# Batch 0's products in a ring of five, its stages B and P on other PSUM banks, z written in six pieces, and stage Y and B units of batch 1's time in other slots

## The chip, the cores and the metric

The kernel runs on one core of one Trainium2 chip. The metric is the time on the device in microseconds (us), from the median of several runs. A profiled run gives a trace besides; its span is about 2 us shorter than the time of the same run. Engine names: PE is TensorE, DVE is VectorE, ACT is ScalarE, POOL is GpSimd, SP is the queue that issues nearly all DMA transfers.

## The reference

```python
def _attn_ref(x, filt_r, filt_i):            # x: 8 x 3008 x 256
    X = np.fft.rfft(x, axis=1)
    Y = X * (filt_r + 1j * filt_i)[None]
    return np.fft.irfft(Y, n=x.shape[1], axis=1)

def _moe_ref(x, w_in, w_out):                # 24064 tokens, 256 -> 2048 -> 256
    h = np.maximum(x @ w_in, 0.0)
    return h * h @ w_out
```

A filter in the frequency domain along the sequence, then a feed-forward network (FFN) with a squared ReLU, over eight batches.

## The kernel before

3008 = 64 x 47, so the transform is done by matmuls in stages. The kernel keeps matmul results in a few tiles of one or two banks of PSUM each, which it uses again and again; a stage that takes a tile waits until the stage before it has been read out. For each batch: **A** (short transforms, result `u` to DRAM and back as `ut`), **B** (second transforms), a **product** with the filter on DVE, **P** (back transforms; ACT evicts them, that is, copies them out of PSUM, as `ze`, which is written to DRAM as `z` and read back in four chunks as `zt`), **Y** (last transforms, giving the tokens `yt`). The FFN goes over 47 groups of 512 tokens in eight slots each: a slot is four matmuls `psH` (w_in), eight matmuls `psO` (w_out, of the group before), a ReLU eviction on ACT and a square on DVE. Batch 0 is transformed in a prologue; the transforms of batch b+1 are strewn over the slots of batch b's FFN by a plan.

The parts that matter (cuts marked with `# ...`):

```python
p_prod = ctx.enter_context(tc.tile_pool(name="p_prod", bufs=3))   # 2 KB per partition each
p_ze = ctx.enter_context(tc.tile_pool(name="p_ze", bufs=3))
# ...
def psF(name):      # two banks; stages A, B, P and Y take them in turn (batch 0's P is on psO)
    return pps.tile([128, 512], F32, tag="psF", name=name, bufs=2)
# psO: two tiles of one bank; psH: two tiles of two banks
sPF = p_prod.tile([128, 6, 128], F16, tag="prod", name="sPF")     # sits in one product buffer

def unit_b(b, p):
    ps = psF(f"psB_{b}_{p}")
    # two matmuls, then on DVE:
    prod = p_prod.tile([128, 2, 2, D], F16, tag="prod", name=f"prod_{b}_{p}")
    nc.vector.tensor_mul(out=prod, in0=..., in1=sF[:, :, 2 * p:2 * p + 2, :])

def fft_plan(b):                       # put(slot, place, unit, ...); place 0 is before psO
    if b == 1:
        for n in range(4, 16):         # the rest of batch 0's stage Y
            put(n - 1 if n < 8 else 10 + n // 2 if n < 12 else 4 * n - 31, n % 2, unit_y, 0, n)
    # ...
    for p in range(12):
        r = t0 + 19 * p // 11          # t0 = 14 for batch 1
        put(r, 0, unit_b, b, p)
        put(r, 0, unit_s, b, p)
        put(r + 2, 1, unit_p, b, p)
    t0 = 36 if b == 1 else 40
    for c in range(4):
        put(t0, 1, read_z, b, c)

# prologue, after the filter's first parts are placed:
for r in range(14):
    if r < 12: unit_b(0, r)
    if r < 10 and r % 2 == 0: place_f(1, r // 2 + 1, nc.scalar)
    if r in (1, 3): place_f(0, r // 2 + 4, nc.scalar)
    if r >= 2: unit_p(0, r - 2)
    for k in {4: (1,), 7: (2,)}.get(r, ()):
        load_wide(1, k); cast_wide(1, k, nc.gpsimd, nc.gpsimd)   # 1 MB of x for batch 1
    if r == 10: read_z(0, 0, (0,))
read_z(0, 0, (1,))
for k in range(2): load_wout(k)        # 2 MB
read_z(0, 1)
```

## Time and profile before

| | before |
|---|---|
| time, median of 3 runs | 809.09 us (808.6 to 809.66) |
| span of the profiled run | 806.2 us |
| PE busy | 784.3 us |
| first stage Y matmul of batch 0 | 52.43 us |
| slot 0, 8, 14, 18, 39 of the FFN begin at | 54.32, 65.48, 77.66, 89.85, 133.11 us |

How to read it: PE is nearly always busy, so the question is only where its idle time lies and what each piece of it waits for. The begin of a slot is the begin of its first `psH` matmul in the timeline. These begins are a ruler: the difference between two of them, held against the same difference in another trace, tells in which stage time was won.

### The profile page before, as it was taken

The numbers are of one execution on the slowest core, as the hardware profiler recorded it, in microseconds if no ns is written. First come the engines' busy times: TensorE is split into PE (matmuls) and PEld (weight loads), VectorE is DVE, ScalarE is ACT, GpSimd is POOL, SyncE is SP. The second block draws the span as 40 slices with busy tenths as digits, with TensorE's granted clock in tenths as the row PEclk, the third lists the DMA queues.
The fourth block names the chain that finished last, engine by engine and source line by source line (L and its number), as shares of the span: only waits on it lengthen the run. The fifth ranks groups of instructions, "written<-read, shape, count | busy, mean of one in ns | idle before, by whom it ended". The sixth has DMA issues, their size and how long they took to land.

```text
span 806.2 us, 14778 instructions
## 1 busy us (share of the span) xinstructions
PE 784.3 (97%) x6102; PEld 552.4 (69%) x6102; DVE 554.1 (69%) x899; ACT 554.0 (69%) x709; POOL 18.5 (2%) x23
## 2 busy tenths in 40 slices
PE   8879899999999999999999999999999999999997
PEld 5746566767776676866768677776667667676666
DVE  6756896569955798558975599656995579654342
ACT  3756666767767677676767677777777767666663
POOL 3320000000000000000000000000000000000000
PEclk9999999999999999999999999999999999999999
DMA  9895357155543457235671555625563332511111
GB/s 362 315 280 177 91 153 176 55 169 144 154 109 82 142 157 198 65 105 157 163 178 39 174 138 138 155 66 157 143 170 91 98 126 82 128 52 41 40 40 53
DMA packets 88091, 108.10 MB, mean 134 GB/s; under 512 B 6240, under 2 KB 78816, under 8 KB 83552
## 3 DMA queue, kind: packets, MB, share of 16 engines
q1 hardware_dynamic: 87816, 106.98, 46.4%
q8 instruction: 48, 0.79, 0.4%
q10 hardware_dynamic: 144, 0.18, 0.1%
q14 instruction: 19, 0.16, 0.1%
q0 software_dynamic: 64, 0.00, 0.0%
HBM read 58.90 MB, written 48.23 MB: 133 GB/s over the span
## 4 chain that ended last, share of the span: by engine, by line
PE 87%; DMA 6%; DVE 4%; ACT 1%; issue 0%; SPq 0%; ACTq 0%; DVEq 0%
PE psO L549 37%; PE psH L534 36%; DMA zt<-dZ 3%; PE psA L349 3%; PE psB L433 3%; PE psY L504 2%; DMA ut<-dU 2%; PE psP L468 2%; DVE prod L436 2%; DMA dZ<-ze 1%; PE warm L267 1%; PE psf L283 1%; ACT h L538 0%; PE psf L286 0%; DVE h L542 0%
## 5 line engine op out<-in xcount | busy, mean ns | idle before, releaser
L538 ACT ACTIVATE h<-psH 128x1024 f16<-128x1024 f32 x376 | 384.8, 1024 | 193.2 <-PE psH L534 193.2
L534 PE MATMUL psH<-yt,sWin 128*128 128x512 f16 (+7 forms) x1728 | 387.8, 352 | 2.8 <-DVE yt L513 2.2
L549 PE MATMUL psO<-sWout,h 128*128 128x256 f16 x3008 | 388.7, 273 | 0.0
L549 PEld LDWEIGHTS <-h 128*128 128x128 f16 x3008 | 290.2, 98 | 78.2
L542 DVE TENSOR_TENSOR h<-h 128x1024 f16<-128x1024 f16 x376 | 254.3, 685 | 105.6 <-ACT h L538 104.1
L534 PEld LDWEIGHTS <-sWin 128*128 128x128 f16 x1728 | 159.3, 98 | 103.5 <-issue 5.3
L436 DVE TENSOR_TENSOR prod<-psB,sF 128x1024 f16<-128x1024 f32 x96 | 116.6, 1219 | 10.9 <-PE psB L433 7.4
L513 DVE CAST yt<-psY 128x376 f16<-128x376 f32 x64 | 35.0, 549 | 59.3 <-PE psY L504 59.3
L470 ACT CAST ze<-psP 128x512 f16<-128x512 f32 x96 | 55.8, 585 | 22.8 <-PE psP L468 19.4
L355 DVE CAST u<-psA 96x512 f16<-96x512 f32 x50 | 34.3, 687 | 47.3 <-PE psA L349 45.1
L556 ACT COPY ost<-psO 128x512 f32<-128x512 f32 x94 | 55.4, 590 | 8.1 <-PE psO L549 6.4
L504 PE MATMUL psY<-sC,zt 112*128 112x94 f16 x512 | 42.8, 207 | 5.2 <-DMA zt<-dZ 5.2
L504 PEld LDWEIGHTS <-zt 112*128 112x128 f16 x512 | 35.0, 99 | 17.6 <-DMA zt<-dZ 5.6
L433 PE MATMUL psB<-ut,sSB 128*128 128x256 f16 x192 | 36.7, 272 | 3.3 <-DVE prod L436 1.9
L450 DVE TENSOR_TENSOR yf<-prod,yf 128x512 f16<-128x512 f16 x84 | 35.7, 425 | 2.9
L349 PE MATMUL psA<-x,sC 94*96 94x512 f16 x96 | 36.7, 382 | 0.0
L433 PEld LDWEIGHTS <-sSB 128*128 128x128 f16 x192 | 18.6, 97 | 24.9 <-issue 6.2
L468 PE MATMUL psP<-yf,sSP 128*128 128x256 f16 x168 | 32.1, 273 | 1.8 <-DVE prod L436 1.6
L511 ACT CAST yt<-psY 128x376 f16<-128x376 f32 x64 | 29.8, 468 | 3.9 <-PE psY L504 3.9
L328 DVE CAST x<-x 94x2048 f16<-94x2048 f32 x24 | 29.2, 1216 | 0.0
L353 ACT CAST u<-psA 96x512 f16<-96x512 f32 x50 | 28.6, 572 | 0.0
L443 DVE COPY yf<-prod 64x512 f16<-64x512 f16 x84 | 24.3, 289 | 2.9
(59 smaller groups left out, 227.2 us busy)
## 6 DMA issues: line engine op xcount, KB each, us to landing
x<-in_x_dram SPq DMA_DIRECT2D x20, 768.0 KB
dZ<-ze SPq DMA_DIRECT2D x32, 384.0 KB
zt<-dZ SPq DMA_DIRECT2D x64, 192.0 KB
dU<-u SPq DMA_DIRECT2D x28, 384.0 KB
out_dram<-ost SPq DMA_DIRECT2D x32, 256.0 KB
out_dram<-ost SPq DMA_DIRECT2D x64, 128.0 KB
ut<-dU SPq DMA_DIRECT2D x7, 1024.0 KB
xw<-in_x_dram SPq DMA_DIRECT2D x6, 1024.0 KB
```

What stands on the lines that cost most here:

```text
L349: nc.tensor.matmul(ps[0:96, :], sSA, x16s[(b, c)][:, m, :], start=True, stop=True)
L433: nc.tensor.matmul(ps[:, i * D:(i + 1) * D], sSB[:, 2 * p + i, :], uts[b][:, 2 * p + i, :], start=True, stop=True)
L436: nc.vector.tensor_mul(out=prod, in0=ps.rearrange("p (a d) -> p a d", d=D).unsqueeze(1).to_broadcast([128, 2, 2, D]), in1=sF[:, :, 2 * p:2 ...
L450: nc.vector.tensor_add(out=yf, in0=prod[:, 0], in1=yf)
L468: nc.tensor.matmul(ps[:, i * D:(i + 1) * D], sSP[:, c2, :], prod[:, i, :], start=True, stop=True)
L470: nc.scalar.copy(out=zes[(b, c)][:, 2 * i6:2 * i6 + 2, :], in_=ps.rearrange("p (a d) -> p a d", d=D))
L504: nc.tensor.matmul(ps[:, 94 * jj:94 * jj + 94], zt[:, 4 * (g % 2) + jj, dt * 128:(dt + 1) * 128], sSY, start=True, stop=True)
L534: nc.tensor.matmul(ps[:, i, o:o + n], sWin[:, dt, jt * 128:(jt + 1) * 128], yts[b][:, dt, r:r + n], start=(dt == 0), stop=(dt == 1))
L538: nc.scalar.activation(out=h2[:, 2 * s:2 * s + 2, :], in_=ps, func=AF.Relu)
L542: nc.vector.tensor_mul(out=v, in0=v, in1=v)
L549: nc.tensor.matmul(pso[g][:, t % 2, :], h2s[g][:, jt, t * 128:(t + 1) * 128], sWout[:, jt, :], start=(jt == 0), stop=(jt == NJT - 1))
L556: nc.scalar.copy(out=ost, in_=pso[g])
```

## The change

Its intent: let the twelve products of batch 0 follow each other without waiting for stage P, write z sooner, read z ahead of w_out, and take stage Y units out of slots in which DVE is busy with stage B. The core of the diff:

```diff
-    sPF = p_prod.tile([128, 6, 128], F16, tag="prod", name="sPF")
+    sPF = p_out.tile([128, 6, 128], F16, tag="ost", name="sPF")
 def unit_b(b, p):
-        ps = psF(f"psB_{b}_{p}")
+        if b == 0 and p % 4 > 1:
+            ps = psO(f"psB_{b}_{p}").rearrange("p a d -> p (a d)")
+        else:
+            ps = psF(f"psB_{b}_{p}")
+        if b == 0:
+            if p == 0:
+                prods["ring"] = p_y.tile([128, 5, 2, 2, D], F16, tag="yt", name="prods_0")
+            prod = prods["ring"][:, p % 5]
+        else: ...
+    def unit_p0(k):                                   # stage P of batch 0, two products at a time
+        ze = p_ze.tile([128, 6, D], F16, tag="ze", name=f"ze_0_{k}")
+        ps = psH(f"psP_0_{k}")
+        # eight matmuls, one ACT eviction of 1024 columns, one z write of 256 KB
 def unit_y(b, n):
-        if dt == 0:
+        if dt == 0 or (b == 0 and g > 5):             # units 13 and 15 to ACT
 def fft_plan(b):
-                put(n - 1 if n < 8 else 10 + n // 2 if n < 12 else 4 * n - 31, n % 2, ...)
+                put(n - 1 if n < 8 else n + 2 if n < 12 else 2 * n - 7, n % 2, unit_y, 0, n)
-                put(3 + k, 1, cast_wout, k, nc.vector)
+                put(4 + k, 1, cast_wout, k, nc.vector)
-            r = t0 + 19 * p // 11
+            r = t0 + (18 if b == 1 else 19) * p // 11
-        t0 = 36 if b == 1 else 40
+        t0 = 35 if b == 1 else 40
 # ... the prologue's loop goes over pairs of products with unit_p0; then
     read_z(0, 0, (1,))
-    for k in range(2):
-        load_wout(k)
     read_z(0, 1)
     for c in (0, 2, 1):
         chunk_a(1, c)
+    for k in range(2):
+        load_wout(k)
```

More of the change, by code (lines that the diff above doesn't have):

```diff
@@ L434, in unit_b @@
                              uts[b][:, 2 * p + i, :], start=True, stop=True)
-        prod = p_prod.tile([128, 2, 2, D], F16, tag="prod", name=f"prod_{b}_{p}")
+        if b == 0:
+            if p == 0:
+                prods["ring"] = p_y.tile([128, 5, 2, 2, D], F16, tag="yt", name="prods_0")
+            prod = prods["ring"][:, p % 5]
+        else:
+            prod = p_prod.tile([128, 2, 2, D], F16, tag="prod", name=f"prod_{b}_{p}")
         nc.vector.tensor_mul(
@@ L453 @@
     sSPx = []
+    def unit_p0(k):
+        ze = p_ze.tile([128, 6, D], F16, tag="ze", name=f"ze_0_{k}")
+        ps = psH(f"psP_0_{k}")
+        for i in range(4):
+            c2 = 4 * k + i
+            prod = prods[(0, c2 // 2)]
+            for v, w in enumerate((sSP[:, c2, :], sSPx[c2 // 12][:, c2 % 12, :])):
+                nc.tensor.matmul(ps[:, i // 2, (i % 2) * D:(i % 2) * D + D], w,
+                                 prod[:, v, i % 2, :], start=(v == 0), stop=(v == 1))
+        nc.scalar.copy(out=ze[:, 0:4, :], in_=ps.rearrange("p t (a d) -> p (t a) d", d=D))
+        nc.sync.dma_start(
+            out=dZ[0].rearrange("(s p) d -> p s d", p=128)[:, 4 * k:4 * k + 4, :],
+            in_=ze[:, 0:4, :])
     def unit_p(b, p):
@@ L458, in unit_p @@
             zes[(b, c)] = p_ze.tile([128, 6, D], F16, tag="ze", name=f"ze_{b}_{c}")
-        prod = prods.pop((b, p))
-        ps = psO(f"psP_{b}_{p}").rearrange("p a d -> p (a d)") if prologue[0] else psF(f"psP_{b}_{p}")
+        yf = prods.pop((b, p))
+        ps = psF(f"psP_{b}_{p}")
         for i in range(2):
-            c2 = 2 * p + i
-            if b == 0:
-                for v, w in enumerate((sSP[:, c2, :], sSPx[c2 // 12][:, c2 % 12, :])):
-                    nc.tensor.matmul(ps[:, i * D:(i + 1) * D], w, prod[:, v, i, :],
-                                     start=(v == 0), stop=(v == 1))
-            else:
-                nc.tensor.matmul(ps[:, i * D:(i + 1) * D], sSP[:, c2, :], prod[:, i, :],
-                                 start=True, stop=True)
+            nc.tensor.matmul(ps[:, i * D:(i + 1) * D], sSP[:, 2 * p + i, :], yf[:, i, :],
+                             start=True, stop=True)
         nc.scalar.copy(out=zes[(b, c)][:, 2 * i6:2 * i6 + 2, :],
@@ L584, in fft_plan @@
             for n in range(4, 16):
-                put(n - 1 if n < 8 else 10 + n // 2 if n < 12 else 4 * n - 31, n % 2,
-                    unit_y, 0, n)
+                put(n - 1 if n < 8 else n + 2 if n < 12 else 2 * n - 7, n % 2, unit_y, 0, n)
             for k in range(4):
-                put(3 + k, 1, cast_wout, k, nc.vector)
+                put(4 + k, 1, cast_wout, k, nc.vector)
         t0 = 2 if b == 1 else 6
@@ L656 @@
     cast_wide(1, 0, nc.gpsimd, nc.gpsimd)
-    for r in range(14):
-        if r < 12:
-            unit_b(0, r)
-        if r < 10 and r % 2 == 0:
-            place_f(1, r // 2 + 1, nc.scalar)
-        if r in (1, 3):
-            place_f(0, r // 2 + 4, nc.scalar)
-        if r >= 2:
-            unit_p(0, r - 2)
-        for k in {4: (1,), 7: (2,)}.get(r, ()):
-            load_wide(1, k)
-            cast_wide(1, k, nc.gpsimd, nc.gpsimd)
-        if r == 10:
+    for k in range(7):
+        if k < 6:
+            unit_b(0, 2 * k)
+            if k < 5:
+                place_f(1, k + 1, nc.scalar)
+            unit_b(0, 2 * k + 1)
+        if k > 0:
+            unit_p0(k - 1)
+        if k < 2:
+            place_f(0, k + 4, nc.scalar)
+        if k in (2, 3):
+            load_wide(1, k - 1)
+            cast_wide(1, k - 1, nc.gpsimd, nc.gpsimd)
+        if k == 5:
             read_z(0, 0, (0,))
     read_z(0, 0, (1,))
-    for k in range(2):
-        load_wout(k)
     read_z(0, 1)
```

## The prediction

> **What bounds the kernel now.** I read the page first (busy shares, the forty slices), then a table of windows for the first 200 us, then the chain of waits and the timeline of the windows in which TensorE idles.
>
> ```profile
> PE 784.3 (97%) x6102; PEld 552.4 (69%) x6102; DVE 554.1 (69%) x899; ACT 554.0 (69%) x709; POOL 18.5 (2%) x23
> ...
> PE   8879899999999999999999999999999999999997
> ```
>
> TensorE (PE) is busy for 784.3 of 806.2 us, so all of its idle time is 21.9 us (2.7%). It lies in the prologue and the first FFN groups; from 200 us to 700 us PE has under 1 us of gaps. Per FFN slot (four matmuls psH, eight psO) the timeline repeats every 1.74 us (129.63, 131.37, 133.11). The change leaves batches 2 to 7 alone, so it can only win gaps before about 140 us.
>
> First gap, the end of the prologue, from the chain of waits (start us, us, what):
>
> ```profile
> 42.02 2.36 DVE prod L436 x2
> ...
> 44.42 0.62 PE psP L465 x4
> 45.07 0.59 ACT ze L470
> 45.68 3.45 DMA dZ<-ze
> 49.20 0.31 SPq L486
> 49.60 0.38 SPq L316
> 50.03 0.57 SPq L316
> 50.65 1.43 SPq L486
> 52.12 8.59 DMA zt<-dZ
> 60.85 0.33 PE psY L504 x4
> ```
>
> Batch 0's twelve products on VectorE (DVE), stage P, the last z write and the z reads form one chain; the reads of z chunk 1 stand behind the 2 MB of w_out (L316). The timeline shows why the products take 16.4 us (27.93 to 44.38) and not 12 x 1.18 = 14.2:
>
> ```profile
> 30.99 1.23 DVE L436 TENSOR_TENSOR prod<-psB,sF 128x1024 f16<-128x1024 f32 x1 [0.71 <-PE psP L465]
> ...
> 35.34 0.38 PE L433 MATMUL psB<-ut,sSB 128*128 128x256 f16 x2 [0.72 <-DVE prod L436]
> ```
>
> The third product waits for stage P of the first: sPF holds one of the three product buffers until the filter is placed. The waits table of that window has 2.0 us of this in four places. Second, PE idles 2.0 us before z chunk 0 arrives at 52.4, and the clock then drops (columns: PE, PEld, DVE, ACT, POOL busy, clock, DMA):
>
> ```profile
> 51.00:52.00 1.00, 0.00 (x0) 0.00 (x0) 0.53 (x1) 0.00 (x0) 0.00 (x0) 1.00 0.90 205
> 52.00:53.00 1.00, 0.57 (x10) 0.57 (x11) 0.00 (x0) 0.15 (x1) 0.00 (x0) 0.86 1.08 347
> 53.00:54.00 1.00, 1.00 (x15) 1.00 (x14) 0.55 (x1) 0.53 (x2) 0.00 (x0) 0.50 1.05 329
> 54.00:55.00 1.00, 0.95 (x6) 0.33 (x4) 0.55 (x1) 0.27 (x1) 0.00 (x0) 0.50 1.06 348
> ```
>
> It stays at 0.50 until about 56.1. Third, stage B of batch 1 in slots 14 to 35:
>
> ```profile
> 85.39 0.81 PE L534 MATMUL psH<-yt,sWin 128*128 128x512 f16 x3 [1.64 <-DVE yt L513]
> ...
> 116.17 0.38 PE L468 MATMUL psP<-yf,sSP 128*128 128x256 f16 x2 [1.56 <-DVE prod L436]
> ...
> 135.13 0.49 PE L504 MATMUL psY<-sC,zt 112*128 112x94 f16 x8 [1.00 <-DMA zt<-dZ]
> ```
>
> Here DVE is 90% busy and late: group 2's first matmul waits for stage Y unit 11, put in slot 15 beside two stage B units; later stage P waits for a product; then batch 1's stage Y waits for z.
>
> **What the Trainium skill says.** "TensorE: Matmul & The Clock Gate", What's actually happening: the clock is halved or full, judged over a free-running window of about 3.4 us. The trace agrees: about 3.2 us at 0.50. But gaps of 1.64 and 1.56 us elsewhere dropped nothing, so a slightly shorter gap may escape. "Perfetto Trace Analysis", Optimization Strategy: consistent bubbles can mean too few buffers; the waits for stage P are such. "DMA: Bandwidth & Descriptors", Queues, rings and completion order: each engine consumes a ring's descriptors in order, so reads queued behind w_out wait; 8.59 us here against 3.49 for a z read at 131.50. "VectorE: DVE Perf Modes", The perf-mode tier table: a two-tensor op with a PSUM operand runs at the lowest rate; the row of L436 has 1219 ns for 1024 elements, and nothing in the change makes it shorter.
>
> **The change part by part.**
> 1. Ring of five, four banks for stage B. The first product still starts at 27.9 (it waits for ScalarE's (ACT) filter eviction). With 12 x 1.18 us back to back, the last ends near 42.2, not 44.4. The rival limit is ACT: eight filter evictions less two done, and now six wide stage P evictions of about 1.02 us for twelve of 0.585 (7.0 to 6.1 us). Walking the order (filter, filter, P by turns, two shared banks) I get each product's bank and filter ready 0.5 to 1 us ahead, so the DVE sets the pace. Stage P of the last pair then ends near 42.7, its eviction near 43.9; before, 45.66. Gain 1.7.
> 2. Six z writes of 256 KB for four of 384 KB. Same bytes, earlier start, a shorter last one. But DMA is at 0.7 to 1.0 share from 35 to 48 us with three 1 MB loads of x, and three z buffers for six writes is a new wait: the sixth eviction needs the third write landed. A write issued at 38.73 landed only at about 44.0, so the third may land at 43.3 and cost 0.5. I put the last landing at 47.5 instead of 49.13, and the first stage Y at 50.7 instead of 52.43: gain 1.7.
> 3. w_out behind z chunk 1. That read now lands near 51.5, before slot 3 wants it. In the old trace the fourth h eviction ended at 60.47 and the fifth began at 62.08, with a 0.47 us yt eviction between: gain 1.1. w_out lands near 57, still before slot 8.
> 4. Clock. PE ends stage A of batch 1 near 48.5, and idles about 2 us still. At half rate for 3.2 us, 1.6 us are lost; I give 45% that the window escapes: 0.7 expected.
> 5. Units 8 to 11 in slots 10 to 13 instead of 14 and 15. Slots 14 to 17 took 89.85 - 77.66 = 12.2 us; their matmuls need 4 x 1.74, three B and two P of 0.22, five Y of 0.17: 8.9. The 3.3 lost should fall to about 0.3: gain 3.0. Slots 10 to 13 have DVE and ACT to spare.
> 6. Units 13 and 15 on ACT take 2 x 0.5 us off DVE; stage B in 18 steps instead of 19 adds pressure: slots 27 to 30 have three B units and two x casts, on DVE 4.05 + 2.92 + 0.65 + 4.05 = 11.7 us against 8.3 us of PE. Before, slots 18 to 38 lost 2.2 us (43.3 against 41.1). I expect 1.2 to stay: gain about 1.0.
> 7. z of batch 1 read one slot earlier (35). One slot is 1.74 us and the wait was 1.00 plus about 0.3 after it: gain 1.2.
>
> Sum: 1.7 (parts 1 and 2 are one chain, counted once) + 1.1 + 0.7 + 3.0 + 1.0 + 1.2 = 8.7 us. After slot 40 all is PE-bound and unchanged, so it passes to the end: 809.1 - 8.7 = 800.4, which I round to 800.6.
>
> **The rivals.**
> (a) The prologue is bound by transfers, not by products: the same bytes must pass, xw loads wait for GpSimd casts, and the last z write lands hardly earlier. For it: the DMA share near 1.0. Against: the share sinks to 0.7 and less at 31 to 39 us, which earlier writes can fill, and it is idle at 48 to 50. Then parts 1 to 4 bring 1.5: 803.
> (b) DVE remains the bound in stage B and denser spacing moves the stall instead of removing it (a new wait for h or a product near slot 30). For it: the 11.7 against 8.3. Against: four stage Y evictions, 2 us, leave that stretch, and stage P may lag two slots. Then parts 5 to 7 bring 3: 803.
> (c) The idle gap shortens enough that the clock stays full and PE starts warm: another 0.9: 799.7, and if the stalls of stage B vanish altogether, 798.
> (d) A moved transfer hurts: z chunks 2 and 3 or w_out late for slot 10 or 8. Slot 10 comes near 67 us and the transfers end near 65, so I do not expect it: 803 to 804.
>
> **Range and chances.** The prologue is uncertain by some 1.7 either way, stage B by 1.5, runs by 0.5 (808.6 to 809.66). So 797.8 to 803.8. Two per cent is 16 us, three quarters of all PE idle time: faster 0.02. Slower needs a loss of 16 us from moves of buffers: 0.01.
>
> **What would show it.** Part 1: products without waits for psP, spanning about 14.3 us from 27.9. Part 2: last z write near 44, first psY near 50.7. Part 3: no wait for zt at slot 3. Part 4: clock in the us windows after the first psY. Part 5: no wait of psH for yt near slot 16; slots 14 to 17 in about 9.2 us. Part 6: waits for DVE between slots 27 and 34 under 1.3 us. Part 7: no psY wait for zt near 127. It is wrong if the last z write lands at 49 still, if a stall above 2 us appears in slots 27 to 34, or if stage B or later batches shift a bank's wait elsewhere.

## The result, and the profile after

The changed kernel takes 800.09 us (median of 4 runs, 799.05 to 802.09) against 808.85 us (median of 4 runs) for the kernel before. The ratio is 0.9894, with a 95% interval from 0.9873 to 0.9916. Ratios here and below are the mean time of one kernel's runs over that of the other's of the same rounds, so not quite the ratio of the medians. Executions over 1.5% slower than the fastest of the same kernel are left out of the means. The gain is 1.1%, under the two per cent of which the prediction speaks.

The page of the changed kernel, its first busy line and its PE row:

```profile
PE 782.8 (98%) x6102; PEld 553.3 (69%) x6102; DVE 552.7 (69%) x897; ACT 554.3 (69%) x705; POOL 18.5 (2%) x23
...
PE   8979999999999999999999999999999999999998
```

PE idles 15.7 us of 798.5 now, 6.2 us less than before, and is busy 1.5 us less; together that is the 7.7 us between the two spans. The ruler tells where:

| stretch | before | after | won |
|---|---|---|---|
| start to slot 0 | 54.32 | 54.29 | 0.03 |
| slot 0 to 8 | 11.16 | 8.88 | 2.28 |
| slot 8 to 14 | 12.18 | 13.26 | -1.08 |
| slot 14 to 18 | 12.19 | 8.58 | 3.61 |
| slot 18 to 39 | 43.26 | 41.13 | 2.13 |
| slot 39 to 42 | 8.42 | 7.69 | 0.73 |
| slot 42 to the end | 664.67 | 664.67 | 0 |

Slots 14 and 18 as lines of the two timelines, before and then after:

```profile
77.66 1.03 PE L534 MATMUL psH<-yt,sWin 128*128 128x512 f16 x4
...
89.85 1.02 PE L534 MATMUL psH<-yt,sWin 128*128 128x512 f16 x4
```

```profile
76.43 1.03 PE L551 MATMUL psH<-yt,sWin 128*128 128x512 f16 x4
...
85.01 1.02 PE L551 MATMUL psH<-yt,sWin 128*128 128x512 f16 x4
```

The sum is 7.70 us, the whole difference of the two spans. The first row is the surprise: the part of the change that was meant to end the prologue sooner moved its end by nothing. One trace is one draw, though: the five kept traces with the old prologue (the kernel before, plan_only, y811_only, dense_only and y1215_only) begin slot 0 between 53.17 and 55.17 us and slot 8 between 64.86 and 66.05. The changed kernel, ze6 and ze6_read begin slot 8 between 62.80 and 63.17. So the gain up to slot 8 is clear of this scatter, and "nothing" means nothing within about 1 us. The timelines of DVE and of ACT in the changed kernel show both sides of it:

```profile
27.17 4.62 DVE L444 TENSOR_TENSOR prods<-psB,sF 128x1024 f16<-128x1024 f32 x4 [1.06 <-ACT sF L293]
32.00 9.14 DVE L444 TENSOR_TENSOR prods<-psB,sF 128x1024 f16<-128x1024 f32 x8 [0.21 <-PE psB L436]
```

```profile
44.32 1.01 ACT L473 CAST ze<-psP 128x1024 f16<-128x1024 f32 x1 [3.58 <-DMA dZ<-ze]
```

The twelve products now come in two runs with 0.21 us between, and end at 41.14 instead of 44.38. But the sixth eviction of stage P then waits 3.58 us for a buffer whose write has not landed. The chain of waits, from the third eviction to the first stage Y:

```profile
36.16 1.00 ACT ze L473
37.17 7.05 DMA dZ<-ze
44.32 1.02 ACT ze L473
45.36 4.06 DMA dZ<-ze
49.44 3.27 DMA zt<-dZ
52.84 0.33 PE psY L521 x4
```

A write of 256 KB takes 7.05 us to land. Before, the corresponding last write was issued at 45.68; now it is issued at 45.36. While it waits, PE has nothing either (it needs x for batch 1, which lands late too), and its clock is halved; in the windows below the last three columns are the granted clock, the DMA share and GB/s:

```profile
42.00:43.00 1.00, 0.01 (x1) 0.00 (x0) 0.00 (x0) 0.00 (x0) 0.00 (x0) 0.93 0.88 341
43.00:44.00 1.00, 0.00 (x0) 0.00 (x0) 0.00 (x0) 0.00 (x0) 0.42 (x1) 0.50 1.10 413
...
50.00:51.00 1.00, 1.00 (x6) 0.56 (x5) 0.86 (x2) 0.15 (x1) 0.00 (x0) 1.00 0.43 106
```

This slow phase (42.9 to 49.7) falls on stage A of batch 1, whose last matmul ends at 52.3, just ahead of z at 52.8, so it should cost little (argued, not tested); and at the first stage Y the clock is full again, where before it was halved there. In slots 14 to 42 the whole list of PE waits over 0.2 us is now three lines:

```profile
84.80 0.38 PE L485 MATMUL psP<-yf,sSP 128*128 128x256 f16 x2 [0.21 <-ACT yt L528]
...
128.65 0.70 PE L521 MATMUL psY<-sC,zt 112*128 112x94 f16 x8 [0.26 <-ACT yt L528]
130.07 0.63 PE L551 MATMUL psH<-yt,sWin 128*128 128x64 f16 x5 [0.31 <-DVE yt L530]
```

The waits of psH for yt (1.64 us), of stage P for a product (1.56 us) and of stage Y for z (1.00 us), all three shown in the prediction, are gone.

### The profile page after: what moved, and what is told of

Same layout as the page of the kernel before. It is cut to its first block, busy times and chain, and to the rows that moved or that the text cites. A ratio compares the mean times of both kernels' runs of the same rounds, so it can differ in the third digit from the quotient of the medians.

```text
span 798.5 us, 14777 instructions
## 1 busy us (share of the span) xinstructions
PE 782.8 (98%) x6102; PEld 553.3 (69%) x6102; DVE 552.7 (69%) x897; ACT 554.3 (69%) x705; POOL 18.5 (2%) x23
## 4 chain that ended last, share of the span: by engine, by line
PE 90%; DMA 7%; ACT 1%; DVE 1%; SPq 0%; issue 0%; ACTq 0%
PE psO L566 40%; PE psH L551 39%; PE psY L521 3%; PE psA L349 3%; PE psB L436 3%; PE psP L485 2%; DMA sPF<-cPF 2%; DMA ut<-dU 2%; DMA dZ<-ze 2%; DMA zt<-dZ 1%; PE psf L283 1%; PE psf L286 1%; ACT h L555 1%; ACT sF L293 0%; ACT ze L473 0%; DVE yt L530 0%
## 5 line engine op out<-in xcount | busy, mean ns | idle before, releaser
L444 DVE TENSOR_TENSOR prod<-psB,sF 128x1024 f16<-128x1024 f32 x84 | 102.5, 1220 | 6.4 <-PE psB L436 6.1
L487 ACT CAST ze<-psP 128x512 f16<-128x512 f32 x84 | 49.2, 585 | 17.9 <-PE psP L485 16.0
```

What stands on the lines that cost most here:

```text
L444: nc.vector.tensor_mul(out=prod, in0=ps.rearrange("p (a d) -> p a d", d=D).unsqueeze(1).to_broadcast([128, 2, 2, D]), in1=sF[:, :, 2 * p:2 ...
L487: nc.scalar.copy(out=zes[(b, c)][:, 2 * i6:2 * i6 + 2, :], in_=ps.rearrange("p (a d) -> p a d", d=D))
```

## The experiments

Twelve kernels ran, all correct, in three sets, each set on one chip and beside runs of the kernel before. Four undo or isolate parts of the change; four go after the third z write; four test the clock, one single slot and a version that follows from the rest.

### The two halves of the change apart: prologue_only and plan_only

```diff
 # prologue_only: the changed kernel, with fft_plan and the eviction rule of unit_y as before
 # plan_only: the kernel before, with the changed fft_plan and eviction rule
```

> The batch 0 parts alone (ring, four banks, six z writes, w_out behind z chunk 1), with the old placing of stage Y, B and z reads for batch 1. Theory from the two traces: the six-write z ring eats what the product ring wins (first psY no earlier than 52), so only the slot 3 wait and the clock remain: gain 2.3 us, 806.5. The recorded prediction's sum for these parts: 3.5 us, 805.3. If the gain is under 1 us, the placing of batch 1 turns it into longer waits later.

> The old prologue with the new placing for batch 1 (stage Y units 8 to 15, B in 18 steps, z read at 35, cast_wout one slot later). Theory: the two halves add, so this one brings about 5.7 us, 803.1, with no psH wait for yt at slot 16 and no DVE wait near slot 30. Rival: VectorE stays the bound and without the earlier prologue the stall moves: gain 3 us or less, 806.

prologue_only: 807.27 us against 807.76 us, ratio 0.9983 (0.9968 to 0.9997), over five runs. Its remaining run, the profiled one, took 3268.72 us: its `psO` matmuls took 744 ns on average instead of 273, while the recorded clock stood at 1.0. Nothing is concluded from that trace, and nothing explains it. plan_only: 803.17 us, ratio 0.9942 (0.9930 to 0.9955); the set's own trace agrees, with slots 14 to 18 in 8.59 us and 18 to 39 in 41.13, the same as in the changed kernel.

What follows: most of the gain is the plan's. By the ratio the prologue's part is about 1.4 us (0.0017 x 808), nearer to the 2.3 us of the traces than to the 3.5 us predicted, but its interval (0.2 to 2.6 us) holds both my theory and less. The two ratios multiplied give 0.9925, a little short of 0.9894, within the intervals. In the traces the changed kernel reaches slot 42 2.6 us ahead of plan_only (133.83 against 136.44), of which 0.9 us is that run's later start of slot 0; but in plan_only's trace the clock stood at 0.50 for some 6.8 us, where it did so for 3.4 us in the kernel before, so this is one draw too. plan_only met its expectation (803.1).

### The plan's parts: y811_only and dense_only, y1215_only

```diff
 # y811_only, in the kernel before:
-                put(n - 1 if n < 8 else 10 + n // 2 if n < 12 else 4 * n - 31, n % 2, unit_y, 0, n)
+                put(n - 1 if n < 8 else n + 2 if n < 12 else 4 * n - 31, n % 2, unit_y, 0, n)
 # dense_only, in the kernel before:
-            r = t0 + 19 * p // 11
+            r = t0 + (18 if b == 1 else 19) * p // 11
-        t0 = 36 if b == 1 else 40
+        t0 = 35 if b == 1 else 40
 # y1215_only, in the kernel before:
-                put(n - 1 if n < 8 else 10 + n // 2 if n < 12 else 4 * n - 31, n % 2, unit_y, 0, n)
+                put(n - 1 if n < 8 else 10 + n // 2 if n < 12 else 2 * n - 7, n % 2, unit_y, 0, n)
```

> Only stage Y units 8 to 11 in slots 10 to 13 instead of 14 and 15. Theory: slots 14 to 17 lose their 3.3 us of stalls and slots 10 to 13 need 0.7 us more in place of 14 and 15, which is no loss: gain 2.5 to 3.3 us, 806. Rival (VectorE is simply overloaded in slots 14 to 33): the stall comes back at slots 27 to 30, gain under 1.2 us, 807.8.

> Only stage B in 18 steps and z read at slot 35, stage Y where it was. Theory: the z wait of 1.0 us at slot 39 goes, but with units 13 and 15 still on VectorE the denser steps add about as much stall: between 1 us better and 1 us worse than 808.9. Rival (density costs nothing): 1.2 to 2 us better.

> The kernel before with only stage Y units 12 to 15 in slots 17, 19, 21, 23 instead of 17, 21, 25, 29 (13 and 15 still evicted by VectorE). Theory: the 1.56 us wait of stage P at slot 29 came from unit 15 there, which made stage P wait for the bank of the product just issued; it goes: slots 18 to 39 take 41.5 to 42 us instead of 43.3, gain 1.3 to 1.8 us, 806.5. Rival (VectorE is overloaded by stage B and the x casts at 28 and 31): the wait stays, gain under 0.5 us.

y811_only: 805.01 us, ratio 0.9963 (0.9950 to 0.9977), 3.0 us won. Slots 14 to 18 took 8.59 us and slots 18 to 39 took 43.25, exactly as in the kernel before. So the early stall did not come back later, as it would if DVE were simply overloaded over the whole stretch. Of PE's waits in that trace, these two remain:

```profile
113.38 0.38 PE L468 MATMUL psP<-yf,sSP 128*128 128x256 f16 x2 [1.56 <-DVE prod L436]
132.59 0.49 PE L504 MATMUL psY<-sC,zt 112*128 112x94 f16 x8 [1.25 <-DMA zt<-dZ]
```

dense_only: 805.83 us, ratio 0.9972 (0.9959 to 0.9985), 2.3 us won. This missed what I expected (between 1 us better and 1 us worse) and met the rival's 1.2 to 2 us and more. The z wait went, as both theories said; but the 1.56 us wait near slot 29 shrank too, although stage B stood denser and units 13 and 15 were still on DVE. PE's waits there:

```profile
85.70 0.81 PE L534 MATMUL psH<-yt,sWin 128*128 128x512 f16 x3 [1.63 <-DVE yt L513]
...
115.19 0.38 PE L468 MATMUL psP<-yf,sSP 128*128 128x256 f16 x2 [0.32 <-DVE prod L436]
```

So load on DVE was not what made that wait. The timeline of the kernel before, slot 29, shows what did:

```profile
113.16 1.22 DVE L328 CAST x<-x 94x2048 f16<-94x2048 f32 x1
113.18 0.38 PE L433 MATMUL psB<-ut,sSB 128*128 128x256 f16 x2
113.40 1.04 PE L549 MATMUL psO<-sWout,h 128*128 128x256 f16 x8
114.27 0.33 PE L504 MATMUL psY<-sC,zt 112*128 112x94 f16 x4
114.30 0.68 DVE L542 TENSOR_TENSOR h<-h 128x1024 f16<-128x1024 f16 x1
114.90 1.21 DVE L436 TENSOR_TENSOR prod<-psB,sF 128x1024 f16<-128x1024 f32 x1
```

Stages B, Y and P take the two psF banks in turn. In slot 29 the order is B (unit 9), Y (unit 15), P (unit 8). Stage P therefore gets the bank that stage B filled 3 us earlier, and must wait for that product, which stands on DVE behind an x cast and a square and ends at 116.11; P starts at 116.17. P's own input had been ready since 112.65. Of the old plan's slots only this one has the order B, Y, P. In dense_only slot 29 has no B unit, in the changed plan Y units 14 and 15 come at slots 21 and 23, where no P follows a B and a Y.

y1215_only was made to test this alone. By time it is unclear: 807.26 us, ratio 0.9980 (0.9959 to 1.0001). By the trace the wait at slot 29 is gone, and slots 18 to 39 take 42.11 us instead of 43.26, a little less gain than I expected. And it makes a small copy of the same wait elsewhere: with unit 13 in slot 19 that slot has now the order B, Y, P.

```profile
91.71 0.38 PE L433 MATMUL psB<-ut,sSB 128*128 128x256 f16 x2
91.93 1.04 PE L549 MATMUL psO<-sWout,h 128*128 128x256 f16 x8
92.80 0.33 PE L504 MATMUL psY<-sC,zt 112*128 112x94 f16 x4
93.41 0.38 PE L468 MATMUL psP<-yf,sSP 128*128 128x256 f16 x2 [0.27 <-DVE prod L436]
```

There no x cast stands before the product, and the wait is 0.27 us. The order in a slot makes the wait, what stands ahead of the product on DVE sets its length. The load on DVE isn't free of blame altogether: y1215_only keeps another wait of 0.38 us at 121.87, of `psO` for a square behind an x cast. So of the 2.13 us that the changed plan wins in slots 18 to 39, this run puts 1.15 down to the order; the rest goes with the denser steps and the units on ACT, which were not taken apart further.

### The third z write: ze6, ze6_read, xw_only, ze6_read_xw

```diff
 # ze6, in the changed kernel (six z buffers; the product buffers are free in the prologue now):
-        ze = p_ze.tile([128, 6, D], F16, tag="ze", name=f"ze_0_{k}")
+        if k < 3:
+            ze = p_ze.tile([128, 6, D], F16, tag="ze", name=f"ze_0_{k}")
+        else:
+            ze = p_prod.tile([128, 4, D], F16, tag="prod", name=f"ze_0_{k}")
 # ze6_read, besides: the first z read behind the last write
-        if k == 5:
-            read_z(0, 0, (0,))
+    read_z(0, 0, (0,))
     read_z(0, 0, (1,))
 # xw_only, in the changed kernel: the first x load of batch 1 into a buffer free at 21 us
-        pool = p_h2 if (b, k) == (0, 2) else p_x32
+        pool = p_h2 if (b, k) in ((0, 2), (1, 0)) else p_x32
 # ze6_read_xw: all of these
```

> The changed kernel, with writes 3 to 5 of z from the three product buffers that batch 0 no longer uses, so no stage P eviction waits for an earlier write. Theory A (buffers): the 3.58 us wait of the last eviction goes, but the last write is issued behind the first z read, which waits for the third write: last write at about 44.7 instead of 45.4, first psY at 52, gain 0.5 us against the changed kernel. Theory B (transfers): the third write still lands at 44 and all transfers end at 48.5, first psY at 52.8, gain 0.

> As ze6, with the first half of the read of z chunk 0 issued after the last write. Theory A: last write issued at 42.8, lands by 46.5 to 47.5, first psY near 50.5: gain 1.5 to 2 us against the changed kernel. Theory B: the queue of transfers is full from 33 to 48.5 us whatever the order, the last write lands at 48.5 or later, first psY at 52: gain under 0.7 us.

> The changed kernel with the first 1 MB load of x for batch 1 in a buffer that is free at 21 us, so it is issued some 6 us earlier and fills the idle DMA stretch at 29 to 32 us; z buffers as in the changed kernel. Theory B: all later transfers land about 3 us earlier, the third z write by 41, the last by 46.5, first psY near 50: gain 2 to 3 us. Theory A: the ring of three still couples eviction and landing; the wait shrinks to 1 us, gain 1 us.

> All three: six z buffers, the read behind the last write, x earlier. If buffers and transfers both bind, this is the best: last write near 42.8, landing by 45.5, first psY near 48.8, gain 3.5 to 4 us against the changed kernel, 796.3. If only transfers bind, it equals xw_only within 0.7 us.

The question is whether the three z buffers (theory A) or the transfers themselves (theory B) hold the end of the prologue.

| | time, us | ratio to before | first psY | slot 8 |
|---|---|---|---|---|
| changed kernel | 800.09 | 0.9894 | 52.84 | 63.17 |
| ze6 | 800.09 | 0.9901 | 52.54 | 62.87 |
| ze6_read | 800.76 | 0.9913 | 52.47 | 62.80 |
| xw_only | 800.34 | 0.9904 | 51.57 | 63.16 |
| ze6_read_xw | 800.75 | 0.9909 | 51.69 | 63.39 |

None is faster than the changed kernel, so the gains expected of xw_only (2 to 3 us by theory B, 1 by theory A) and of all three together (3.5 to 4) were missed. In ze6 and ze6_read the 3.58 us wait is gone (the sixth eviction runs at 41.73 and 42.22), and z arrives 0.3 to 0.4 us earlier, no more than the scatter of the traces: theory B. So the visible wait of ACT was not the cause by itself, it only stood in front of a transfer that would have been late anyhow. xw_only does bring z 1.3 us earlier, and then slot 8 begins at the same time. Its windows say why:

```profile
50.00:51.00 1.00, 0.00 (x0) 0.00 (x0) 0.00 (x0) 0.00 (x0) 0.00 (x0) 1.00 1.10 238
...
53.00:54.00 1.00, 0.98 (x3) 0.41 (x3) 0.33 (x1) 0.00 (x0) 0.00 (x0) 0.50 1.06 307
54.00:55.00 1.00, 1.00 (x4) 0.30 (x2) 0.00 (x0) 0.08 (x1) 0.00 (x0) 0.50 1.05 343
55.00:56.00 1.00, 1.00 (x4) 0.34 (x3) 0.02 (x1) 0.95 (x1) 0.00 (x0) 0.50 1.10 357
```

With x earlier, stage A of batch 1 ends earlier too, PE idles 2.8 us before z, and the clock is halved over the first slots. What the transfers won, the clock took.

### The clock by itself: before_warm

```diff
 # in the kernel before, ahead of the first stage Y:
+    ps = psF("warm2")
+    for _ in range(10):
+        nc.tensor.matmul(ps, zero, s1[:, 0:6, :].rearrange("p w q -> p (w q)")[:, 0:512],
+                         start=True, stop=True)
```

> The kernel before with ten more 512-column matmuls of zeros (2.2 us) between stage A of batch 1 and the first stage Y, where TensorE idled 2.0 us and its clock then stood at 0.50 for 3.2 us. Theory (the halved clock costs): clock 1.0 throughout, first h eviction near 54.9 instead of 56.40, slot 8 about 0.7 to 1.4 us earlier: 1 us faster than before. Rival (slots 0 to 8 are held by ScalarE and the z read of chunk 1, the clock hides behind them): slot 8 within 0.4 us of before, no gain.

It took 810.14 us, ratio 1.0020 (1.0001 to 1.0039): no gain, the rival's case and slightly worse. The extra matmuls did hold the clock at 1.00, and the first h eviction came at 54.32 instead of 56.40. But then:

```profile
58.00:59.00 1.00, 0.00 (x0) 0.00 (x0) 1.00 (x3) 0.39 (x1) 0.00 (x0) 1.00 1.02 263
59.00:60.00 1.00, 0.00 (x0) 0.00 (x0) 0.41 (x1) 0.00 (x0) 0.00 (x0) 1.00 1.13 337
60.00:61.00 1.00, 0.93 (x8) 0.58 (x9) 0.00 (x0) 0.47 (x1) 0.00 (x0) 1.00 1.15 347
61.00:62.00 1.00, 1.00 (x8) 0.49 (x6) 0.47 (x2) 0.70 (x1) 0.00 (x0) 0.61 1.09 353
62.00:63.00 1.00, 1.00 (x4) 0.30 (x3) 1.00 (x3) 0.32 (x1) 0.00 (x0) 0.50 1.09 315
```

PE runs into the wait for z chunk 1, which stands behind w_out and arrives near 60 us (60.07 here, 60.85 in the kernel before); it idles 2.7 us, and the clock is halved after that. In the kernel before, the slow clock was hidden behind the late chunk 1, so the full clock alone wins nothing. The reverse doesn't hold. xw_only has w_out moved and the slow clock at the first slots; its slots 0 and 8 begin here:

```profile
53.02 4.26 PE L551 MATMUL psH<-yt,sWin 128*128 128x512 f16 x12 [0.28 <-ACT yt L528]
...
63.16 0.38 PE L551 MATMUL psH<-yt,sWin 128*128 128x512 f16 x1 [0.15 <-ACT h L555]
```

That is 10.14 us, against 11.16 before and 8.88 in the changed kernel. So of the 2.28 us of slots 0 to 8 about 1.0 belong to w_out alone and about 1.3 to the clock once w_out is out of the way. These are estimates from single traces, in which the slow phases don't cover quite the same part of the slots.

### A version from these results: early_xw, and early_xw_warm

If theory B holds, the x loads must leave the way of the z writes. All three are issued ahead of the first write:

```diff
 # early_xw: ze6_read_xw, and the loads and casts of x parts 1 and 2 hoisted
-        if k in (2, 3):
-            load_wide(1, k - 1)
-            cast_wide(1, k - 1, nc.gpsimd, nc.gpsimd)
+        if k < 2:
+            load_wide(1, k + 1)
+            cast_wide(1, k + 1, nc.gpsimd, nc.gpsimd)
         if k > 0:
             unit_p0(k - 1)
 # early_xw_warm: besides, eight zero matmuls as in before_warm
```

> The changed kernel, with all three loads of x for batch 1 issued ahead of the z writes (the first in a buffer free at 21 us), six z buffers and the first z read behind the last write. Theory B (the last z write lands late because it stands behind the 1 MB loads): the loads end by 40, the last write lands by 45.5, first psY near 48.5; if the clock holds, slot 8 at 59.5 and 796.5; if it halves, 798. Theory C (a write of 512-byte rows takes 4 us to land whatever precedes it): first psY at 50.5, 799.

> As early_xw with eight matmuls of zeros (1.7 us) before the first stage Y. If the halved clock is what ate the gain of the earlier z in the two variants with the early first load (first psY at 51.6, yet slot 8 at 63.2 as before), this is 0.8 to 1.5 us faster than early_xw where that one shows clock 0.50 after the first psY, and equal where it does not.

early_xw takes 797.01 us (796.82 to 797.63), ratio to before 0.9856 (0.9836 to 0.9876), and its slowest run is below the fastest of both kernels; early_xw_warm takes 797.73 us, ratio 0.9863. The end of the prologue in the chain of waits of early_xw:

```profile
42.37 1.02 ACT ze L476
43.39 0.02 issue
43.41 2.33 DMA dZ<-ze
45.74 0.02 issue
45.76 3.15 DMA zt<-dZ
48.90 0.14 issue
49.04 0.33 PE psY L524 x4
```

The last write of z lands in 2.33 us, where it took 4.06 and the third one 7.05. It is the same 256 KB of 512-byte rows, so theory C falls. ze6_read_xw is the closest neighbour: it differs only in that the second and third load of x, with their casts, come later: they are issued at 35.22 and 37.84 instead of 31.43 and 33.91. Its first stage Y is at 51.69, 2.65 us later than here. Whether a write waits for a load that is ahead of it in the rings, or only shares the DMA engines with it, these runs don't tell apart. The first stage Y comes at 49.04 instead of 52.84, PE idles only 0.96 us before it, the clock stays at 1.00, and slot 42 begins at 130.18 instead of 133.83: 3.65 us in the traces, 3.1 by the ratios (0.0038 x 808; by the two intervals an estimated 2.4 us either way). The changed kernel and early_xw did not run on the same chip; each was compared with the kernel before beside it. The zero matmuls add nothing, as expected where the clock holds anyway.

## Why the prediction was right, and where it was not

The predicted total, 800.6 us, was met (800.09). (Its own sum gives 800.4; the step to 800.6 is no rounding, but it changes nothing.) Point by point the sum is partly luck, as two terms were off in opposite directions.

- **Steps 1 and 2** (ring and z writes, one chain, 1.7 us): wrong. The products did come back to back, 13.97 us from first to last where 14.3 was said. The failing step is "I put the last landing at 47.5 instead of 49.13". It landed at 49.44. I had seen the new wait of the sixth eviction for the third write and gave it 0.5 us; it is 3.58. The term is 0.0. My rival (a), transfers, was the true one: ze6 shows that more buffers alone win nothing, early_xw against ze6_read_xw that earlier loads of x do. What I held against it, a DMA share of "0.7 and less at 31 to 39 us", was misread: 0.72 is the mean from 30 to 40 us, and by the microsecond the share is 0.00 at 31, 0.36 at 35 and 0.80 to 1.18 otherwise, so there was little room for earlier writes.
- **Step 3** (w_out, 1.1) and **step 4** (clock, 0.7 expected): 1.8 together, 2.28 measured, of which xw_only puts about 1.0 down to w_out and 1.3 to the clock. The wait for chunk 1 is gone. For the clock the gain came by another way than the 45% allowed for: the gap before z did not escape the window; PE went cold earlier, during the late x, and was warm again in time. before_warm shows that the clock's part can't be had without w_out's, and I had added the two as if they were independent. (The slow phase in the kernel before lasted 3.4 us by its windows, not 3.2.)
- **Step 5** (units 8 to 11): 3.0 said, 2.53 in the traces (3.61 in slots 14 to 18, less 1.08 in slots 8 to 14, where the units now stand and need 0.7), 3.0 by y811_only. Right in mechanism and size.
- **Step 6** (denser stage B): 1.0 said, 2.13 measured. I let 1.2 us of stall stay by comparing DVE's 11.7 us of work with PE's 8.3 us in four slots. None stayed. That the old stall was a matter of load was the wrong step: the 1.56 us of it were the bank order B, Y, P in slot 29, as y811_only, dense_only and y1215_only show together. Rival (b) falls with this: the denser steps brought no new stall.
- **Step 7** (z of batch 1 a slot earlier): 1.2 said, 0.73 measured between slots 39 and 42. The wait for z is gone; the small waits for yt behind it partly stay.

By stage, then, the prediction's 8.7 us stand against 0.03 + 2.28 + 2.53 + 2.13 + 0.73 = 7.70 us in the pair of traces (steps 1 and 2, 3 and 4, 5, 6, 7). The medians of the timed runs differ by 808.85 - 800.09 = 8.76 us; the 1 us between the two figures is of the size of the spread of the runs, so it is not put down to any step.

## What to carry to other kernels

Ask of a late transfer what was issued before it, before you give it more buffers: here six z buffers alone brought the first stage Y 0.3 us forward, and with the loads of x issued ahead of the writes besides it came 3.8 us sooner. Where several stages share a small ring of banks, write down the order in which they take it, slot by slot; a wait for an engine that looks overloaded may be one unit in the wrong place. And don't add gains that lie one behind the other: a full clock won nothing while chunk 1 was late, and a z that came 1.3 us earlier won nothing by slot 8 where the clock fell for it.

## What the Trainium skill lacked or had wrong

- "TensorE: Matmul & The Clock Gate", Why this matters for your kernels, advises no idle gaps over about 3 us. Here gaps of 1.86 us (ze6_read_xw), 2.04 us (kernel before) and 2.81 us (xw_only) were followed by a clock of 0.50, and gaps of 1.64 and 1.56 us (kernel before) and even one of 2.79 us (y1215_only, from 57.44) were not. So a gap of 2 us is already a risk, and its length alone doesn't decide. In the changed kernel the clock fell about 0.85 us after PE had gone idle (42.01), behind three windows in which PE was only 0.61 to 0.80 busy. The page's free-running window of about 3.4 us (What's actually happening) fits the length of the slow phases, about 3.4 us before and 6.8 us after.
- "DMA: Bandwidth & Descriptors", Queues, rings and completion order, has the ring order, but no figure for what it costs a small write. Here a 256 KB write landed in 2.33 us after the loads of x had landed (early_xw), and another of the same size and rows in 7.05 us among 1 MB loads (changed kernel).
- "Perfetto Trace Analysis", Optimization Strategy, speaks of consistent bubbles from too few buffers. No page that I read says that the order in which stages take a ring of PSUM banks can make a single one: 1.56 us in one slot, 0.27 us in another.
- No page explains the one run of 3268.72 us, 4.05 times the median of its kernel, in which matmuls were slower (744 ns for 273) at a recorded clock of 1.0. "TensorE: Matmul & The Clock Gate", Seeing it yourself, knows of a throttle seen stuck at a quarter for 50 us and more, and says that such records can't be fully trusted; no run here shows which it was.
